# Low parts of the MLP and output weights stored in DRAM ahead of use, and two copies of x written later, in a fused attention and MLP kernel

## The chip, the cores and the metric

The kernel runs on one core of a Trainium2 chip. The metric is the device time of one execution in microseconds (us). An engine is one of five: PE (TensorE, the matrix engine), DVE (VectorE), ACT (ScalarE), POOL (GpSimd) and SP (SyncE, which here issues every DMA). Each engine runs its own instructions strictly in the order in which they stand in its queue and waits on semaphores for the others.

## The reference

A layer with x of 2048 rows and 640 columns (16 tiles of 128 rows, four blocks b = 0..3 of 512 rows), 32 heads of 20 columns, an attention window of 256 positions, and an MLP of width 1536 whose activation is a squared ReLU:

```python
x = A_x
xn = _layernorm(x, axis=-1)
s = _A_ref(xn, A_wqkv, A_wo)
g = _silu(_B_ref(xn, B_w1, B_b1, B_w2, B_b2))
return x + s * g
```

`_A_ref` is `softmax(mask(q k^T / sqrt(20))) v`, then the product with `wo`. `_B_ref` is `h = x w1 + b1`, `h = max(h, 0)^2`, `h w2 + b2`.

## The kernel before

Every product is made of parts. A float32 operand is split into a high part, which is a rounded copy made by ACT, and a low part, which is the difference raw minus high, made by a subtraction; a product is then high by high, high by low and low by high, three matmuls. So each weight exists twice in SBUF, as `hi` and `lo`.

**First stage (0 to 118 us of the profile).** For each block b of x: the products for q and k of the first head group (`qk_group`, L200), the next block's normalisation, transposes and split into `xT[0]` and `xT[1]`, and then the value products of all heads, `v_all` (L242). `v_all(b)` makes eight tiles t0..t7 of 15 matmuls each. A tile takes one of three PSUM buffers in turn (t6 has the buffer of t3), and ACT and DVE empty it: ACT L246 copies the high part `vt<-vps`, DVE L247 subtracts (`r<-vps,vt`), and after both the buffer is free; ACT L250 and DVE L251 make the two lower parts. `spill_x(b)` (L160) writes both parts of a block of x to the DRAM copies `xs`, 1280 KB each, since SBUF's place for x is given up before the MLP has used all of it. Stores of a tile are put in `stores`, and `store_all` posts them. In block 3, eight `pair_loads` (L403, 240 KB each) fetch q and k of the first pair of heads back in another layout, just before `v_all(3)`.

**Steps (118 to about 845 us).** Sixteen pairs of heads by 16 query tiles give 256 steps, and a few more to drain. Step s computes the scores of tile s (`sps`, L431), their maxima on DVE (L443), and 9 steps later (`LAG`) the transposed scores (`stps`, L475) with the maxima folded in as additional rows of the operand `qs`. Those rows (`mrow`) are made once for every four tiles (`max_rows`, L461) and reach `qs` by two small DMAs (`post`, L541). The transposed scores of step 9 are the first that read the rows of tiles 0 to 3, those of step 11 the first that read the rows of tiles 4 to 7. Then come the exponentials (ACT L482), the window's selection (POOL L483, L485), a high copy `ph` (ACT L490), a low part `pl` (DVE L496), and the product with the values (`ops`, L510).

**Filler.** Between these, PE gets filler in fixed portions: q and k products of the later head groups (`qkps`, L561), the MLP's first products (`hps`, L561) and second products (`yps`, L823), for half 0 of the MLP's width with blocks n = 0..3 and for half 1 with blocks n = 4..7, and at the end the output products (`wops`). The weights of the filler come in pieces (`piece_lin`, `piece_pair`): a DMA of the raw piece (L643), at least two steps later ACT's copy (L655 for w1 and w2, L663 for q, k and wo) and DVE's subtraction (L658, L664). `tick` releases one piece in a step, `ensure` releases what is left, `issue` starts pieces and, after them, the DMAs of the list `bulk` at a rate per step.

**What sets the order.** In the first stage a scheduler interleaves the engines' instructions; from the first step on (`manual_schedule`) the instructions stand in the order in which the code is written. SP issues DMAs in one order of its own, and eight semaphores go round: a DMA is issued only after the one eight places before it is done.

Of the kernel before, what the change touches and what calls it, by code (L numbers as in the profile page):

```python
# [51 lines left out]
def attn_mlp_kernel(ctx: ExitStack, tc, x, wqkv, wo, w1, b1, w2, b2, out):  # L52
# [15 lines left out]
    def qk_stores(w, rows, cols, hm, lo):  # L68
# [4 lines left out]
        rep = [hm[:, a, :].unsqueeze(1).to_broadcast([P, 3 - a, n]) for a in range(2)]  # L73
        return [(dst[:, 0:3, :], rep[0]), (dst[:, 3:5, :], rep[1]), (dst[:, 5, :], lo)]
    v_d = dram.tile([P, NP, NB, 4 * 2 * VW], BF16, name="v_d")
    y_d = [dram.tile([P, NT, D], F32, name=f"y{i}") for i in range(2)]
    o_d = [dram.tile([4, P, D], F32, name=f"o_{g}") for g in range(NB)]

# [48 lines left out]
    with tc.tile_pool(name="ph1v", bufs=2) as p1v, tc.tile_pool(name="ph1", bufs=2) as p1, tc.tile_pool(name="ph1x", bufs=4) as p1b, tc.tile_pool(name="ph1w", bufs=1) as p1w:  # L127
# [62 lines left out]
        def store_all():  # L190
            for dst, src in stores:
                nc.sync.dma_start(dst, src)
            stores.clear()
# [21 lines left out]
        def norm_jobs(b):  # L215
# [9 lines left out]
                    load_x(b + 1)  # L225
            return [lambda: None] + [lambda t=t: stats(xts[b][t], mv[:, t, :]) for t in range(4)] + [lambda: norm(0), lambda: norm(2)]

        def v_all(b, between=None):
            late = []
            jobs = norm_jobs(b + 2) if b + 2 < NB else []  # L230
            for nh in range(2):
                if nh and between:
                    between()
                vt = p1v.tile([P, NP // 2, 4, 2, VW], BF16, tag="vt", name="vt")
                nc.gpsimd.memset(vt[:, :, :, :, VW - 1:VW], 1.0)
                for t in range(4):
                    ps = pmm.tile([P, HALF], F32, tag="mm", name="vps")
                    n = 0
                    for c in range(KC):
                        for xp, wp in ((0, 0), (0, 1), (1, 0)):  # L240
                            n += 1
                            nc.tensor.matmul(ps, xT[xp][b][:, c * BT + t * P: c * BT + (t + 1) * P], wv[wp][:, c, nh * HALF:(nh + 1) * HALF], start=n == 1, stop=n == 3 * KC)  # L242
# [3 lines left out]
                    nc.scalar.activation(dst[:, :, :, 0:DH], psv, AF.Copy)  # L246
# [12 lines left out]
                late.pop()()  # L259
                stores.append((v_d[:, nh * (NP // 2):(nh + 1) * (NP // 2), b, :], vt.rearrange("p a t h w -> p a (t h w)")))  # L260

        E_ = mybir.EngineType
        with tc.manual_schedule(engines={E_.PE, E_.Activation, E_.DVE, E_.Pool, E_.SP}):
# [103 lines left out]
            for b in range(NB):  # L367
                def next_x():
                    if b + 1 < NB:
                        alloc_x(b + 1)  # L370
                        transpose_chunks(b + 1, xns)
                        xns.clear()
                        store_all()
                        spill_x(b + 1)

                if b == 0:
                    inv_std(rstd1, mv1[:, :, 1])
                    xns = [normalize(xts[1][t], mv1[:, t, :], rstd1[:, t:t + 1]) for t in range(4)]
                    load_x(2)
                    spill_x(0)  # L380
                    nc.sync.dma_start(b1t, b1.rearrange("(c p) -> p c", p=P))
                    nc.sync.dma_start(b2t, b2.partition_broadcast(P))
                    ones_rows(0)
                    raws = [load_w(group_src(1, w), KC) for w in "qk"]
                    v_all(b, next_x)
                    continue
                lasts = []
                for w in "kq":
                    ps = pmm.tile([P, BT], F32, tag="mm", name="qkps")
                    qk_group(w, b, ps)  # L390
                    lasts.append(qk_evac(w, b, ps))
                for f in lasts:
                    f()
                next_x()
                if b == 1:
                    for w in "qk":
                        ws1[w] = group_tiles(1, w)
                        split_w(*ws1[w], raws.pop(0))
                if b == NB - 1:
                    store_all()  # L400
                    for half in range(2):
                        for dst, src in pair_loads(0, half):
                            nc.sync.dma_start(dst, src)  # L403
                v_all(b)
            store_all()


    at1 = ctx.enter_context(tc.tile_pool(name="at1", bufs=1))
# [121 lines left out]
        return rest  # L530


    state = [0.0, 0.0, 0]
    posts = []

    def post(dst, src):
# [35 lines left out]
    def lin1(tiles, off, n):  # L572
        t, o = divmod(off, KC * BT)
        return tiles[t][:, o:o + n]
# [54 lines left out]
    def ensure(tag):  # L629
        flush()  # L630
        while any(p[0] == tag for p in started) or any(p[0] == tag for p in queue):
            start_pieces()
            for f in release(1, True):
                f()
                held[0] -= 1

    def piece(tag, src, go):
        def start():
# [7 lines left out]

    RAWN = {"g": D, "1": FHALF, "2": D, "o": D}

    def piece_lin(tag, tiles, ohi, olo, src):
        n = src.shape[-1]  # L650

        def go(raw):
            t_ = tiles()
            for ap, o, m in lin(t_, ohi, n):
                nc.scalar.activation(ap, raw[:, o:o + m], AF.Copy)  # L655
            cuts = sorted({o for o in range(0, n + 1, P) if (ohi + o) % (KC * BT) == 0 or (olo + o) % (KC * BT) == 0} | {0, n})
            for c0, c1 in zip(cuts, cuts[1:]):
                nc.vector.tensor_sub(lin1(t_, olo + c0, c1 - c0), raw[:, c0:c1], f32(lin1(t_, ohi + c0, c1 - c0)))  # L658
        piece(tag, src, go)

    def piece_pair(tag, hi, lo, src):
        def go(raw):
            nc.scalar.activation(hi(), raw, AF.Copy)  # L663
            nc.vector.tensor_sub(lo(), raw, f32(hi()))  # L664
        piece(tag, src, go)

    def lazy(make):
        got = []
# [17 lines left out]
    def queue_w1(hf):  # L686
        wt = lazy(lambda: [bigp.tile([P, KC * BT], F32R, tag="big", name=f"w1_{hf}_{j}") for j in range(3)])
        for c in range(KC):
            piece_lin(f"1{hf}", wt, c * FHALF, (KC + c) * FHALF, w1[c * P:(c + 1) * P, hf * FHALF:(hf + 1) * FHALF])
        return wt  # L690

    def queue_w2(hf):
        wt = lazy(lambda: [bigp.tile([P, KC * BT], F32R, tag="big", name=f"w2_{hf}_{j}") for j in range(3)])
        for j in range(NFH):
            piece_lin(f"2{hf}", wt, j * D, (NFH + j) * D, w2[hf * FHALF + j * P:hf * FHALF + (j + 1) * P, :])
        return wt

    def load_xb(b):
# [4 lines left out]
    def filler():  # L703
# [50 lines left out]
        for n, (hf, b) in enumerate(blocks):  # L754
            if n % NB == 0:
                ensure(f"1{hf}")
            if n == NB - 1:
# [38 lines left out]
            if n == NB:  # L796
                load_yin(0)
            wt2 = w2t[hf]()
            for tt in range(4):
                t = b * 4 + tt  # L800
                ysb = wgt.tile([P, D], F32, tag="wgqh", name="ysb")
# [30 lines left out]
                if n == last and tt % 2:  # L832
                    load(0)
                    load(1)
            if n == NB - 1:
                shut.discard("21")
        ensure("o")
# [20 lines left out]
    def queue_wo():  # L858
        wob = lazy(lambda: [bigp.tile([P, KC * BT], F32R, tag="big", name=f"wo{j}") for j in range(2)])
        wo4 = lazy(lambda: [wgt.tile([P, FHALF], F32R, tag="wraw", bufs=RAW, name=f"wo4{w}")[:, :D] for w in "hl"])  # L860

        def wo_part(p, c):
            return wob()[p][:, c * D:(c + 1) * D] if c < 4 else wo4()[p]

        for c in range(KC):
            piece_pair("o", lambda c=c: wo_part(0, c), lambda c=c: wo_part(1, c), wo[c * P:(c + 1) * P, :])
        return wo_part

    def out_filler(wo_part):
# [79 lines left out]
    per = total / (steps - 1)  # L949
    with tc.manual_schedule(engines={E_.PE, E_.Activation, E_.DVE, E_.Pool, E_.SP}):  # L950
        load_v(0)
        exs, phs, norm, loads = {}, {}, [], []

        def at_step(n):
# [2 lines left out]
        for s in range(steps):  # L957
# [40 lines left out]
                exs[b] = (exps(*b, *stp), stp[1])  # L998
            if c:
                high(*c, *exs.pop(c))  # L1000
            while norm:
                norm.pop()()
            fill((1 - EARLY_FILL) * per + SWING * (-1) ** (s - LAG - 3))
# [36 lines left out]
```

## Time and profile before

| | |
|---|---|
| median of 3 runs | 929.25 us (929.11 to 930.05) |
| profiled execution, its own time | 928.72 us |
| its span in the profile | 927.0 us |
| first stage, products of the last value block end at | 118.1 us |
| granted TensorE clock | 1.0 |

Times in the profile start at the span's first instruction. "Busy" of an engine is the time in which an instruction of its ran; idle time is put down to what released the engine afterwards. A window is a stretch of the span, with the busy time of each engine and the number of its instructions, the granted clock, the share of the 16 DMA engines' time and the bytes moved. A group is all instructions of one line, engine and operation, with their count, sum, mean duration, and the idle time just before them.

### The profile page before, as it was taken

The numbers are of one execution on the slowest core, as the hardware profiler recorded it, in microseconds if no ns is written. First come the engines' busy times: TensorE is split into PE (matmuls) and PEld (weight loads), VectorE is DVE, ScalarE is ACT, GpSimd is POOL, SyncE is SP. The second block draws the span as 40 slices with busy tenths as digits, with TensorE's granted clock in tenths as the row PEclk, the third lists the DMA queues.
The fourth block names the chain that finished last, engine by engine and source line by source line (L and its number), as shares of the span: only waits on it lengthen the run. The fifth ranks groups of instructions, "written<-read, shape, count | busy, mean of one in ns | idle before, by whom it ended". The sixth has DMA issues, their size and how long they took to land.

```text
span 927.0 us, 21775 instructions
## 1 busy us (share of the span) xinstructions
PE 902.9 (97%) x7632; PEld 728.9 (79%) x7632; DVE 754.8 (81%) x2031; ACT 670.1 (72%) x1282; POOL 530.0 (57%) x832
## 2 busy tenths in 40 slices
PE   8999999999998899999999999999999999999998
PEld 8999976666675578688688678688788687789998
DVE  7875478989989988988888899987888988875554
ACT  5454349888988886987986987977987977984221
POOL 6010017887877875775865875875864965871000
PEclk9999999999999999999999999999999999999999
DMA  6899776776778453253255143365274264055873
GB/s 230 279 398 338 229 249 203 224 240 213 237 234 258 120 187 112 88 181 117 72 180 166 52 149 122 101 222 157 53 253 129 74 220 134 24 189 172 287 277 114
DMA packets 130803, 168.79 MB, mean 182 GB/s; under 512 B 44100, under 2 KB 91268, under 8 KB 128132
## 3 DMA queue, kind: packets, MB, share of 16 engines
q1 hardware_dynamic: 130692, 167.39, 55.3%
q8 instruction: 60, 0.98, 0.4%
q14 instruction: 51, 0.42, 0.2%
HBM read 96.15 MB, written 70.91 MB: 180 GB/s over the span
## 4 chain that ended last, share of the span: by engine, by line
PE 74%; DVE 10%; ACT 5%; issue 4%; DMA 3%; POOL 3%; SPq 1%; POOLq 0%; DVEq 0%; ACTq 0%
PE yps L823 15%; PE hps L561 13%; PE wops L561 8%; PE vps L242 7%; PE qkps L561 7%; PE sps L431 7%; PE ops L510 7%; PE stps L475 6%; DVE junk L443 3%; PE qkps L200 2%; ACT p L482 2%; DVE pl L496 2%; DVE w L658 2%; ACT ph L490 1%; PE otp L889 1%
## 5 line engine op out<-in xcount | busy, mean ns | idle before, releaser
L482 ACT ACTIVATE p<-stps,ebias 128x384 f32<-128x384 f32 (+2 forms) x512 | 258.3, 557 | 82.6 <-PE stps L475 69.4
L443 DVE CUSTOM_DVE_ANT_0 junk<-sps,mask 128x384 bf16<-128x384 f32 (+2 forms) x512 | 251.1, 527 | 62.4 <-PE sps L431 55.2
L496 DVE TENSOR_TENSOR pl<-p,ph 128x768 f16<-128x768 f32 (+2 forms) x256 | 241.3, 943 | 2.6 <-ACT ph L490 2.2
L483 POOL TENSOR_SCALAR_AFFINE_SELECT p<-p 128x256 f32<-128x256 f32 x256 | 146.4, 572 | 136.2 <-ACT p L482 131.3
L490 ACT ACTIVATE ph<-p 128x768 f16<-128x768 f32 (+2 forms) x256 | 206.0, 805 | 15.1 <-POOL p L485 13.3
L561 PE MATMUL hps<-xb,w 128*128 128x512 f32 x630 | 198.2, 430 | 0.0
L823 PE MATMUL yps<-w,hh 128*128 128x320 f32 x768 | 197.6, 330 | 0.0
L823 PEld LDWEIGHTS yps<-w,hh 128*128 128x128 f32 x768 | 132.1, 189 | 8.1 <-issue 1.5
L431 PE MATMUL sps<-ks,qs 120*128 120x384 bf16 (+2 forms) x512 | 127.5, 319 | 8.9 <-DVE mt L443 8.8
L561 PEld LDWEIGHTS hps<-xb,w 128*128 128x128 f32 x630 | 113.3, 189 | 21.2 <-issue 0.4
L475 PE MATMUL stps<-qs,ks 122*128 122x384 bf16 (+2 forms) x512 | 124.4, 322 | 3.2 <-ACT p L482 2.1
L823 PE MATMUL yps<-w,hl 128*128 128x320 f32 x384 | 126.6, 330 | 0.0
L782 POOL TENSOR_TENSOR hl<-sq,hh 128x256 fp32r<-128x256 f32 x96 | 104.3, 1087 | 39.1 <-DVE sq L781 27.5
L510 PEld LDWEIGHTS <-ph 128*128 128x128 f16 x1440 | 86.0, 97 | 26.4 <-issue 21.5
L485 POOL TENSOR_SCALAR_AFFINE_SELECT p<-p 128x256 f32<-128x256 f32 x224 | 106.0, 473 | 0.0
L510 PE MATMUL ops<-vp,ph 128*128 128x61 bf16 x1440 | 101.0, 192 | 0.0
L510 PE MATMUL ops<-vp,pl 128*128 128x61 bf16 x1440 | 99.7, 191 | 0.0
L510 PEld LDWEIGHTS <-pl 128*128 128x128 f16 x1440 | 87.8, 97 | 0.0
L823 PEld LDWEIGHTS yps<-w,hl 128*128 128x128 f32 x384 | 72.4, 189 | 5.0 <-issue 2.0
L475 PEld LDWEIGHTS <-ks 122*128 122x128 bf16 x512 | 30.1, 99 | 55.7 <-issue 45.6
L242 PE MATMUL vps<-wv,xT 128*128 128x320 f32 x480 | 72.1, 309 | 0.6 <-POOL wv L179 0.3
L242 PEld LDWEIGHTS vps<-wv,xT 128*128 128x128 f32 x480 | 70.5, 187 | 1.3 <-POOL wv L179 0.6
(116 smaller groups left out, 1476.8 us busy)
## 6 DMA issues: line engine op xcount, KB each, us to landing
ks<-k_d SPq DMA_DIRECT2D x64, 240.0 KB
qs<-q_d SPq DMA_DIRECT2D x64, 240.0 KB
xb<-xs SPq DMA_DIRECT2D x12, 1280.0 KB
xs<-xT SPq DMA_DIRECT2D x8, 1280.0 KB
y<-ysb SPq DMA_DIRECT2D x32, 320.0 KB
q_d<-shm SPq DMA_DIRECT2D x38, 256.0 KB
v_d<-vt SPq DMA_DIRECT2D x8, 976.0 KB
vp<-v_d SPq DMA_DIRECT2D x16, 488.0 KB
```

The costliest lines, as they stand in the source:

```text
L242: nc.tensor.matmul(ps, xT[xp][b][:, c * BT + t * P: c * BT + (t + 1) * P], wv[wp][:, c, nh * HALF:(nh + 1) * HALF], start=n == 1, stop=n = ...
L431: nc.tensor.matmul(ps[:, :nk], qs[i][0:KR, hh, q * P:(q + 1) * P], ks[i][0:KR, hh, k0 * P:k0 * P + nk], start=True, stop=True)
L443: nc.vector.tensor_tensor_reduce(out=junk[:, :nk], in0=r[hh][:, :nk], in1=mask[:, 3 * P - nk:], scale=1.0, scalar=-3.0e38, op0=ALU.add, op ...
L475: nc.tensor.matmul(ps[:, :n], ks[i][0:KR + 2, hh, kb * P:(kb + 1) * P], qs[i][0:KR + 2, hh, kb * P:kb * P + n], start=True, stop=True)
L482: nc.scalar.activation(p32[:, hh, :n], r[hh][:, :n], AF.Exp, scale=SCALE, bias=ebias)
L483: nc.gpsimd.affine_select(p32[:, :, 0:P], p32[:, :, 0:P], pattern=[[0, 2], [1, P]], compare_op=ALU.is_ge, fill=0.0, base=0, channel_multip ...
L485: nc.gpsimd.affine_select(p32[:, :, 2 * P:], p32[:, :, 2 * P:], pattern=[[0, 2], [-1, P]], compare_op=ALU.is_gt, fill=0.0, base=0, channel ...
L490: nc.scalar.activation(ph[:, :, :n], p32[:, :, :n], AF.Copy)
L496: nc.vector.tensor_sub(pl[:, :, :n], p32[:, :, :n], ph[:, :, :n])
L510: nc.tensor.matmul(ot[:, q % 4, hh, :], t[:, hh, (q - k) * P:(q - k + 1) * P], vp[:, k // 4, k % 4, hh, :], start=m == 1, stop=m == 2 * le ...
L561: nc.tensor.matmul(ps, a, b_, start=j == 0, stop=j == n - 1)
L823: nc.tensor.matmul(pss[nh], hs[fc][hp][:, tt * P:(tt + 1) * P], lin1(wt2, (wp * NFH + fc) * D + nh * HALF, HALF), start=fc == 0 and j == 0 ...
```

## The change

The low parts of w1, w2 and wo are no longer subtracted where the filler uses them. They are made earlier, stored in three DRAM tensors, and read from there by a DMA straight into the `lo` place. The high parts are still loaded raw and copied by ACT. The weights of q and k keep their subtraction.

```diff
+    w1lo_d = [dram.tile([P, KC, FHALF], F32, name=f"w1lo{hf}") for hf in range(2)]
+    w2lo_d = [dram.tile([P, NFH, D], F32, name=f"w2lo{hf}") for hf in range(2)]
+    wolo_d = dram.tile([P, KC, D], F32, name="wolo")
...
             for ap, o, m in lin(t_, ohi, n):
                 nc.scalar.activation(ap, raw[:, o:o + m], AF.Copy)
-            cuts = sorted({o for o in range(0, n + 1, P) if (ohi + o) % (KC * BT) == 0 or (olo + o) % (KC * BT) == 0} | {0, n})
-            for c0, c1 in zip(cuts, cuts[1:]):
-                nc.vector.tensor_sub(lin1(t_, olo + c0, c1 - c0), raw[:, c0:c1], f32(lin1(t_, ohi + c0, c1 - c0)))
+            for ap, o, m in lin(t_, olo, n):
+                post(f32(ap), lo_d[:, o:o + m])
...
+    def piece_low(tag, hi, lo, src, lo_d):
+        def go(raw):
+            nc.scalar.activation(hi(), raw, AF.Copy)
+            post(f32(lo()), lo_d)
+        piece(tag, src, go)
```

The low parts of half 0 (12 pieces of 128 by 640, 320 KB each) are made in the first stage, one after each tile of `v_all(2)` (eight) and of the first four tiles of `v_all(3)`. Each loads a piece two ahead, copies on ACT, subtracts on DVE and stores.

```diff
+        def low_split():
+            if lraws:
+                raw, dst = lraws.pop(0)
+                hi = p1b.tile([P, D], F32R, tag="xn", name="whi")
+                lo = p1b.tile([P, D], F32R, tag="xn", name="wlo")
+                nc.scalar.activation(hi, raw, AF.Copy)
+                nc.vector.tensor_sub(lo, raw, f32(hi))
+                stores.append((dst, like(f32(lo), dst)))
+                low_load()
...
                     store_all()
+                    if b >= 2:
+                        low_split()
...
+                if b == 2:
+                    for _ in range(2):
+                        low_load()
                 v_all(b)
```

Those of half 1 (12) and of wo (5) are made among the steps, during the second products of blocks n = 0..2 and n = 4..6, with the subtraction on GpSimd. `low_tick` runs once a step; what is left at block 3 or 7 is made at once by `ensure_lows`.

```diff
+    def low_split():
+        _, raw, dst = lraws.pop(0)
+        hi = wgt.tile([P, FHALF], F32R, tag="wraw", bufs=RAW, name="whi")[:, :D]
+        nc.scalar.activation(hi, f32(raw), AF.Copy)
+        nc.gpsimd.tensor_sub(raw, f32(raw), f32(hi))
+        post(dst, like(f32(raw), dst))
+
+    def low_tick():
+        if lraws and state[2] >= lraws[0][0] + 3 and state[2] % 4 != 3:
+            low_split()
+        if state[3] and not lraws:
+            low_load()
...
+            if n in (NB - 1, last):
+                ensure_lows()
```

The copies of blocks 2 and 3 of x (four DMAs of 1280 KB) leave the first stage and go into the list `bulk` ahead of the first step.

```diff
-                        spill_x(b + 1)
+                        if b == 0:
+                            spill_x(b + 1)
...
         load_v(0)
+        for b_ in range(2, NB):
+            for p_ in range(2):
+                bulk_dma(1.8, xs_d[p_][b_], f32(xT[p_][b_]))
```

**ACT, the last value block.** Before, ACT's queue there held only the evacuations of the eight tiles (`vt<-vps`, then `vt<-r` for the lower part); these are its rows from t0 on:

```order
L246 ACTIVATE vt<-vps 128x8x2x20 x2
L250 ACTIVATE vt<-r_1355 128x8x2x20
L246 ACTIVATE vt<-vps 128x8x2x20
L250 ACTIVATE vt<-r_1374 128x8x2x20
L246 ACTIVATE vt<-vps 128x8x2x20
L250 ACTIVATE vt<-r_1395 128x8x2x20
```

Now the copies `whi` of the last four pieces of half 0 (pieces 8 to 11, counted from 0) stand between them, each waiting for its load `wraw`:

```order
L281 ACTIVATE vt<-vps 128x8x2x20
L258 ACTIVATE whi<-wraw 128x640
L281 ACTIVATE vt<-vps 128x8x2x20
L285 ACTIVATE vt<-r_1416 128x8x2x20
L258 ACTIVATE whi<-wraw 128x640
L281 ACTIVATE vt<-vps 128x8x2x20
L285 ACTIVATE vt<-r_1441 128x8x2x20
L258 ACTIVATE whi<-wraw 128x640
L281 ACTIVATE vt<-vps 128x8x2x20
L285 ACTIVATE vt<-r_1469 128x8x2x20
L258 ACTIVATE whi<-wraw 128x640
```

The first copy of t3 (the fourth `vt<-vps`) is now queued behind the third `whi`, that of piece 10.

**SP, the same place.** These are SP's rows now from the end of the eight pair loads to the two stores of the values; before, the stores of the values followed the pair loads directly:

```order
L441 DMA qs_125<-q_d 120x1024
L250 DMA wraw<-in_B_w_dram 128x640
L208 DMA w2lo_85<-wlo 128x640
L250 DMA wraw<-in_B_w_dram 128x640
L208 DMA w2lo_85<-wlo 128x640 x3
L208 DMA v_d<-vt 128x8x488 x2
```

The loads of pieces 10 and 11 are the two `wraw`, behind all eight pair loads.

**SP, the start of the steps.** These were SP's rows from the load of the first pair's values (`vp`) to the first rows of maxima (`mrow`); `raw` are pieces of the q and k weights of the next head group:

```order
L419 DMA vp_1532<-v_d 128x1952
L643 DMA raw<-in_A_wqkv_dram 128x5x128 x2
L116 DMA ks_1520<-ones 2x16x256
L590 DMA ks_1520<-k_d 120x1024
L590 DMA qs_1519<-q_d 120x1024
L590 DMA ks_1520<-k_d 120x1024
L590 DMA qs_1519<-q_d 120x1024
L541 DMA q_d<-shm 128x2x512
L541 DMA q_d<-slo 128x512
L541 DMA q_d<-shm 128x2x512
L541 DMA q_d<-shm 128x512
L541 DMA qs_120<-mrow 2x4x128 x2
```

and these are they now:

```order
L461 DMA vp_1617<-v_d 128x1952
L632 DMA xs_2_74<-xT_2_758 128x2560
L686 DMA raw<-in_A_wqkv_dram 128x5x128 x2
L632 DMA xs_2_78<-xT_2_759 128x2560
L132 DMA ks_1605<-ones 2x16x256
L632 DMA xs_3_75<-xT_3_1058 128x2560
L583 DMA q_d<-shm 128x2x512
L583 DMA q_d<-slo 128x512
L583 DMA q_d<-shm 128x2x512
L583 DMA q_d<-shm 128x512
L632 DMA xs_3_79<-xT_3_1059 128x2560
L583 DMA qs_125<-mrow 2x4x128 x2
```

All four copies of x stand ahead of the first `mrow`, one of them ahead of `raw`; the four loads of the second pair (`ks`, `qs`) stand behind it, ahead of the second `mrow`.

**DVE, the first weight pieces of the MLP.** Before, a subtraction `w<-raw,w` stood between the low part of the exponentials (`pl`) and the maxima of the next step:

```order
L496 TENSOR_TENSOR pl<-p_4233,ph 128x768
L658 TENSOR_TENSOR w_0_2_4230<-raw,w_0_0_4228 128x768
L443 ISA junk,mt<-sps,mask 128x384
L443 ISA mt 128x1
L443 ISA junk,mt<-sps,mask 128x384
L443 ISA mt 128x1
```

and at the same step now:

```order
L538 TENSOR_TENSOR pl<-p_4321,ph 128x768
L485 ISA junk,mt<-sps,mask 128x384
L485 ISA mt 128x1
L485 ISA junk,mt<-sps,mask 128x384
L485 ISA mt 128x1
```

The subtraction is gone, and the maxima follow `pl` directly.

More of the change, by code (lines that the diff above doesn't have):

```diff
@@ L226, in norm_jobs, with low_load @@
             return [lambda: None] + [lambda t=t: stats(xts[b][t], mv[:, t, :]) for t in range(4)] + [lambda: norm(0), lambda: norm(2)]
+        lows, lraws = mlp_lows(0), []
+        def low_load():
+            if lows:
+                src, dst = lows.pop(0)
+                raw = p1b.tile([P, D], F32, tag="xt", name="wraw")
+                nc.sync.dma_start(like(raw, src), src)
+                lraws.append((raw, dst))
+        def low_split():
[7 more added lines that the diff above has]
+                low_load()
         def v_all(b, between=None):
@@ L403, in attn_mlp_kernel @@
                             nc.sync.dma_start(dst, src)
+                if b == 2:
+                    for _ in range(2):
+                        low_load()
                 v_all(b)
             store_all()
+            assert not lraws
     at1 = ctx.enter_context(tc.tile_pool(name="at1", bufs=1))
@@ L635, in ensure @@
                 held[0] -= 1
+        post_all()
     def piece(tag, src, go):
@@ L647, in attn_mlp_kernel, with piece_lin @@
     RAWN = {"g": D, "1": FHALF, "2": D, "o": D}
-    def piece_lin(tag, tiles, ohi, olo, src):
+    def piece_lin(tag, tiles, ohi, olo, src, lo_d):
         n = src.shape[-1]
@@ L665, in piece_pair, with low_load, ensure_lows @@
         piece(tag, src, go)
+    def piece_low(tag, hi, lo, src, lo_d):
[3 more added lines that the diff above has]
+        piece(tag, src, go)
+    lows, lraws = [], []
+    def low_load():
+        if lows:
+            src, dst = lows.pop(0)
+            raw = wgt.tile([P, FHALF], F32R, tag="wraw", bufs=RAW, name="raw")[:, :D]
+            post(like(f32(raw), src), src)
+            lraws.append((state[2], raw, dst))
+    def low_split():
[9 more added lines that the diff above has]
+            low_load()
+    def ensure_lows():
+        while lows or lraws:
+            if not lraws:
+                low_load()
+            post_all()
+            low_split()
+        post_all()
     def lazy(make):
@@ L756, in filler @@
                 ensure(f"1{hf}")
+            if n == 0:
+                lows.extend(mlp_lows(1))
+            if n == NB:
+                lows.extend((wo[c * P:(c + 1) * P, :], wolo_d[:, c, :]) for c in range(KC))
+            if n in (NB - 1, last):
+                ensure_lows()
             if n == NB - 1:
@@ L798, in filler @@
             wt2 = w2t[hf]()
+            state[3] = n not in (NB - 1, last)
             for tt in range(4):
```

18 lines of the change are left out of this document (14 added, 4 removed).

## The prediction

> **What bounds the kernel now.** I read the page first: the busy shares, then the chain of work that ended last.
>
> ```profile
> span 927.0 us, 21775 instructions
> PE 902.9 (97%) x7632; PEld 728.9 (79%) x7632; DVE 754.8 (81%) x2031; ACT 670.1 (72%) x1282; POOL 530.0 (57%) x832
> PE 74%; DVE 10%; ACT 5%; issue 4%; DMA 3%; POOL 3%; SPq 1%; POOLq 0%; DVEq 0%; ACTq 0%
> ```
>
> PE is busy for 902.9 of 927.0 us, so all its idle time together is 24 us. No edit here changes PE's work, so the change can win only from those 24 us, and loses wherever it makes PE wait. The question is which of the idle time belongs to the subtractions that leave DVE. The second view is therefore the table of windows around the weight pieces:
>
> ```profile
> core 0: us, PE busy (x) PEld busy (x) DVE busy (x) ACT busy (x) POOL busy (x), PEclk, DMA share, GB/s
> 240.00:270.00 30.00, 30.00 (x274) 21.28 (x273) 27.63 (x75) 25.22 (x48) 23.51 (x35) 1.00 0.75 242
> 270.00:300.00 30.00, 26.00 (x215) 17.36 (x213) 28.48 (x65) 26.61 (x48) 21.47 (x29) 1.00 0.77 242
> 300.00:320.00 20.00, 17.13 (x141) 11.41 (x142) 19.90 (x47) 18.09 (x37) 16.10 (x20) 1.00 0.42 131
> 350.00:510.00 160.00, 159.80 (x1496) 127.04 (x1495) 136.51 (x407) 126.56 (x244) 104.54 (x181) 1.00 0.40 128
> 540.00:560.00 20.00, 17.68 (x167) 14.78 (x164) 19.93 (x50) 16.48 (x29) 14.68 (x21) 1.00 0.48 147
> 580.00:600.00 20.00, 18.71 (x163) 12.79 (x163) 19.86 (x53) 19.12 (x39) 16.70 (x23) 1.00 0.40 117
> ```
>
> At 240 to 270 and 350 to 510 PE has next to no idle time. In the four windows where pieces of w1 and w2 are split, DVE is full (28.48 of 30, 19.90, 19.93 and 19.86 of 20) and PE is idle for 4.00, 2.87, 2.32 and 1.29 us: 10.5 us. The waits of PE and the subtraction's share of these windows:
>
> ```profile
> PE sps L431 <- DVE mt L443: 5.2, 9, 1.2
> PE sps L457 <- DVE mp L448: 1.7, 3, 0.7
> 270.00:300.00 30.00, 7.56 (x7) 1.00 0.77 242
> 300.00:320.00 20.00, 6.93 (x6) 1.00 0.42 131
> 540.00:560.00 20.00, 5.97 (x7) 1.00 0.48 147
> 580.00:600.00 20.00, 4.32 (x4) 1.00 0.40 117
> ```
>
> The first two rows are PE's waits from 270 to 320: 6.9 us, all for DVE's maxima, in pieces of at most 1.2 us. The other four are DVE's busy time of the subtraction (L658) alone: 24.8 us in the four windows.
>
> **The gain (G).** 26 subtractions of w1 and w2 leave DVE, at 1035 ns each:
>
> ```profile
> L658 DVE TENSOR_TENSOR w<-raw,w 128x640 fp32r<-128x640 f32 (+3 forms) x26 | 26.6, 1035 | 0.0
> L655 ACT ACTIVATE w<-raw 128x640 fp32r<-128x640 f32 (+3 forms) x24 | 17.4, 734 | 1.0 <-DMA raw<-in_B_w_dram 1.0
> ```
>
> DVE's relief (24.8 us) exceeds what PE idles there (10.5), so the relief itself is not the limit. The next limit is ACT, whose copies stay: it idles 3.39, 1.91, 3.52 and 0.88 us in the four windows, and a window can shrink by no more than the smaller of PE's and ACT's idle time: 3.39 + 1.91 + 2.32 + 0.88 = 8.5 us. With the little that PE idles beyond these windows the bounds are 7 and 10.5; I take **G = 9.0**. The subtractions of wo are not on the path: PE is the full engine there, so nothing is counted.
>
> **The value products (A).** PE's rows of `v_all(2)` and `v_all(3)`, and the DMA traffic of the first of them:
>
> ```profile
> 75.80 17.85 PE L242 MATMUL vps<-wv,xT 128*128 128x320 f32 x120
> 100.35 17.76 PE L242 MATMUL vps<-wv,xT 128*128 128x320 f32 x120
> 64.00:84.00 20.00, 20.00 (x127) 18.72 (x126) 13.57 (x29) 9.34 (x21) 0.80 (x2) 1.00 1.06 393
> 80.00:98.00 18.00, 18.00 (x114) 17.20 (x113) 7.14 (x17) 6.91 (x16) 0.39 (x1) 1.00 0.66 253
> ```
>
> A tile takes 17.8 / 8 = 2.2 us. In `v_all(2)` DVE and ACT have room for eight splits (7.14 and 6.91 busy of 18 us). The queue moved 253 GB/s x 18 us = 4.6 MB from 80 to 98; 2.6 MB of x leave it, eight loads and eight stores of 0.33 MB bring 5.2 MB, together 7.2 MB, or 398 GB/s, against 393 in the fullest window quoted. So it just fits: 0 to 3 us, I take 0.5.
>
> In `v_all(3)` the load of piece 10 stands behind the eight pair loads, and ACT's copy of tile t3 behind the copy of that piece.
>
> ```profile
> 104.99 0.46 SPq L403 DMA_DIRECT2D ks<-k_d  x1
> 108.47 0.42 SPq L403 DMA_DIRECT2D qs<-q_d  x1
> 111.44 0.38 SPq L192 DMA_DIRECT2D v_d<-vt  x1
> DMA  9999999797796988889999999999998421000000
> GB/s 348 330 351 348 333 274 271 195 230 108 108 210 225 323 318 271 292 328 353 343 312 350 346 334 353 383 320 317 303 298 254 137 85 37 7 0 0 0 0 0
> L663 ACT ACTIVATE wgkh<-raw 128x640 fp32r<-128x640 f32 x3 | 2.3, 751 | 0.0
> 109.34 0.46 ACT L246 ACTIVATE vt<-vps 128x320 bf16<-128x320 f32 x1 [1.38 <-PE vps L242]
> 113.74 0.45 ACT L246 ACTIVATE vt<-vps 128x320 bf16<-128x320 f32 x1 [1.61 <-PE vps L242]
> ```
>
> The first three rows are SP issuing the first and the last pair load and the values' store (1.0 MB) behind them; the next two are the DMA engines from 104 to 120 in slices of 0.4 us. The queue is full until 116 and empty at 118. Counting 1.0 MB back from its end puts the end of the pair loads between 113.6 (all of the tail is the store) and 116. Piece 10 takes the store's place: 0.33 MB at about 0.33 MB/us is 1.0 us, so it lands at 114.6 to 117, I take 116. Then come ACT's copy (0.75), DVE's subtraction, which stands ahead of t3's on DVE (1.03), and t3's own subtraction (about 0.5): t3's PSUM buffer is free at 118.3. The last ACT row, at 113.74, is the emptying of t5: PE has finished t5 there and wants that buffer for t6. PE waits 118.3 - 113.7 = 4.6; **A = 4.5 + 0.5 = 5.0**, between 0 (piece 10 lands before 111.5) and 8. Before, t3 was emptied from 109.34 on, so this wait is wholly new. The first scores stand two tiles earlier on PE now, but cost only what they did. Late values also move the store `v_d`, and with it the start of the next part, by the same amount.
>
> **The start of the steps (B).**
>
> ```profile
> xs<-xT SPq DMA_DIRECT2D x8, 1280.0 KB
> 120.00:138.00 18.00, 17.48 (x82) 12.24 (x80) 14.48 (x50) 6.15 (x10) 3.50 (x3) 1.00 0.95 301
> DMA  0069999989999999999968899999999999995038
> 136.90 1.28 SPq L541 DMA_DIRECT2D qs<-mrow  x2
> 138.12 0.50 PE L475 MATMUL stps<-qs,ks 122*128 122x384 bf16 x2
> 142.82 0.50 PE L475 MATMUL stps<-qs,ks 122*128 122x384 bf16 x2
> ```
>
> The second row is the window from 120 to 138, the third the DMA engines from 120 to 140 in slices of 0.5 us. The queue is full from 121.5 on and drains at 138.2, just after the second rows of maxima were issued (136.90). PE needs the first rows at 138.12 (step 9) and the second at 142.82 (step 11), so before there were 4.6 us to spare for the second. Now four copies of 1.31 MB, 5.24 MB, stand ahead of both in SP's order. At 393 GB/s they take 13.3 us; the second rows land at 138.2 + 13.3 = 151.5, and PE waits 151.5 - 142.8 = **8.7 us = B** in all, part of it already at step 6 (the `raw` of the q weights is a copy later, and DVE's subtraction of it stands ahead of the maxima) and at step 9. If the old traffic too ran at 393 GB/s, 5.4 + 5.24 MB would need 27 us from 120.5 on, and the wait would be about 5; if the copies ran at 301, 17.4 us, and 12.8. Nothing makes this good later: PE is the full engine afterwards, and its filler is dealt out in a fixed order.
>
> On such an order the Trainium skill says, under "DMA: Bandwidth & Descriptors", section "Queues, rings and completion order", that descriptors of one issuer's queue are consumed in ring order on each DMA engine, but that completion is not first in, first out across engines, so that a small DMA may be done while a large earlier one still runs. By the first half B stands; by the second it would be near 0 if the few bytes of `mrow` went to engines that are done with their share of the copies. Of the trace, the full row of digits (9 in nearly every slice) shows all 16 engines loaded alike, which speaks for the first.
>
> **Splits among the steps (C).** 17 splits add 734 ns of ACT and one subtraction of POOL each.
>
> ```profile
> L179 POOL TENSOR_TENSOR wgkl<-raw,wgkh 128x640 fp32r<-128x640 f32 x2 | 3.4, 1708 | 6.3 <-DMA raw<-in_A_wqkv_dram 6.3
> L663 ACT ACTIVATE wo4h<-raw 128x640 fp32r<-128x640 f32 x1 | 0.7, 739 | 1.0 <-DMA raw<-in_A_wo_dram 1.0
> ```
>
> That is 12 x 0.73 = 9 us of ACT and 20 us of POOL within 350 to 510, where they idle 33 and 55 us while PE is full: hidden, as long as each load is in when ACT comes to it. One isn't: the twelfth piece of half 1 is loaded and copied at once. The nearest row is ACT's wait of 1.0 for a raw piece; bounds 0.5 and 3, **C = 1.5**. 27 low pieces come by DMA in place of a subtraction, 0.33 MB each; I count nothing for them, but their cover is that DMA has room at 270 to 320 (third rival).
>
> **Sum.** 928.7 (the profiled execution's own time) - 9.0 + 5.0 + 8.7 + 1.5 = 934.9. The median lies 0.5 above that execution, so I forecast **935.4 us**, 0.7% slower.
>
> **The rivals.**
>
> *Faster: the queue has room.* If DMA takes the additional traffic at its best rate everywhere, B is 5 or less and A about 1; G may be 10.5: 929.25 - 10.5 + 5 + 1 + 0.5 = 925. For it: before, the queue drained before every consumer, and 120 to 138 moved only 301 GB/s. Against it: the share there was already 0.95. It decides for faster once A + B falls below 7. Chance 0.16, times 921 to 927.4.
>
> *No difference.* The loads of pieces 10 and 11 land early (A near 1) and B stays at 7 to 8: 929.25 - 9 + 1 + 7.5 + 1.5 = 930. For it: the low end of the window of landing times above. Chance 0.12.
>
> *Slower still: the low parts come late.* From 270 to 320 the queue moved 242 x 30 + 131 x 20 GB/s = 9.9 MB; the low parts of half 0 add 12 x 0.33 = 3.9 MB. 13.8 MB need 35 us at 393 GB/s and 46 at 301, of 50. At the second rate the products `hps` and `yps` wait for DMA where scores waited for DVE, and G is used up: 944. For it: share 0.77 in the busier part. Against it: a piece is read a few steps after it is asked for. Chance 0.12, times 941 to 946.
>
> *The subtractions weren't the bound.* DVE is full there with maxima and `pl` too; if ACT fills up sooner than its idle time says, G is 3 and the time 941. Within the last case's range; it has a part of the forecast's upper end.
>
> **How the numbers follow.** The forecast's own case, 931.1 to 941, has 0.60. A measurement of this kernel tells 0.2%, 1.9 us, from no change: faster 0.16, same 0.12, slower 0.72. The range that leaves out 0.2: 925 (half of the faster case below it) to 942.5 (most of the slowest above it).
>
> **What would show each step.** G: the windows around the weight pieces have DVE below full, and PE's waits for the maxima (6.9 us) are nearly gone. A: PE idle in front of t6, put down to DVE or ACT behind `whi`. B: PE idle at the transposed scores of steps 9 and 11 until `mrow` lands, and a full row of DMA digits to about 150. C: ACT waiting for the last raw piece of half 1. I am wrong if PE is busy without a gap from 118 to 150, or if PE waits from 270 to 320 as before.

## The result, and the profile after

| | before | after |
|---|---|---|
| median of 5 runs | 929.5 us (929.11 to 930.05) | 944.7 us (942.3 to 946.55) |
| profiled execution, its own time | 928.72 us | 942.30 us |
| its span | 927.0 us | 940.6 us |

The ratio is 1.0163, with a 95% interval of 1.0152 to 1.0174: 1.6% slower. The forecast was 935.4 us, 0.7% slower, with a range to 942.5: the direction is right, but the forecast size is less than half of the measured one, and the time lies above the range. The page after, in the lines that were shown of before:

```profile
span 940.6 us, 21946 instructions
PE 907.6 (96%) x7632; PEld 733.2 (78%) x7632; DVE 746.3 (79%) x2012; ACT 683.9 (73%) x1311; POOL 549.1 (58%) x849
PE 77%; ACT 6%; DVE 6%; DMA 6%; SPq 2%; issue 2%; POOL 1%; ACTq 0%; POOLq 0%; DVEq 0%
```

DVE's share of the chain fell from 10% to 6%, as it should without the subtractions; DMA's rose from 3% to 6%. PE runs as many instructions, but was busy for 907.6 instead of 902.9 us: 4.7 us more for the same work. The windows of the two places that were forecast to lose say why, in their column PEclk:

```profile
core 0: us, PE busy (x) PEld busy (x) DVE busy (x) ACT busy (x) POOL busy (x), PEclk, DMA share, GB/s
80.00:98.00 18.00, 18.00 (x115) 17.27 (x114) 10.09 (x20) 8.38 (x18) 0.39 (x1) 1.00 0.95 305
114.00:122.00 8.00, 0.62 (x4) 0.19 (x2) 0.85 (x2) 1.48 (x4) 0.00 (x0) 0.66 0.95 328
122.00:126.00 4.00, 3.57 (x13) 3.57 (x14) 3.25 (x7) 2.21 (x5) 0.00 (x0) 0.50 0.46 176
140.00:160.00 20.00, 15.39 (x64) 10.29 (x62) 10.49 (x36) 8.95 (x14) 5.14 (x7) 0.91 1.03 388
```

PE stands still for nearly all of 114 to 122, and runs at half its clock for some 4 us afterwards. The other thing to see is the first row: beside the values of block 2 the share of the DMA engines' time is 0.95, but they move 305 GB/s, not the 393 that the forecast took.

Where the time went is best read from PE, since the order of its instructions is the same in both kernels but for two scores. The start of the same PE instruction in the two profiles, us:

| PE instruction | before | after | later by | in this part |
|---|---|---|---|---|
| last matmul of `v_all(3)` | 117.80 | 128.77 | 10.97 | **+10.97** (A) |
| transposed scores of step 11 | 142.82 | 162.44 | 19.62 | **+8.65** (B) |
| scores of step 60 | 273.64 | 293.05 | 19.41 | -0.21 |
| scores of step 80 | 336.22 | 352.71 | 16.49 | **-2.92** (half 0's weights) |
| scores of step 140 | 497.43 | 514.43 | 17.00 | +0.51 |
| scores of step 148 | 518.69 | 537.63 | 18.94 | **+1.94** (C) |
| scores of step 180 | 609.25 | 624.35 | 15.10 | **-3.84** (half 1's weights) |
| last transposed scores | 836.33 | 850.32 | 13.99 | -1.11 |

**A** is 11.0 where 5.0 was forecast. Four rows of after show its chain, from SP (the first pair load, and the load of piece 10), ACT (the copy of piece 10) and PE (tiles t6 and t7):

```profile
109.57 0.57 SPq L441 DMA_DIRECT2D ks<-k_d  x1
113.84 0.37 SPq L250 DMA_DIRECT2D wraw<-in_B_w_dram  x1
120.38 0.74 ACT L258 ACTIVATE whi<-wraw 128x640 fp32r<-128x640 f32 x1 [11.96 <-DMA wraw<-in_B_w_dram]
122.43 6.64 PE L277 MATMUL vps<-wv,xT 128*128 128x320 f32 x30 [6.12 <-DVE r L282]
```

The kind of wait is the forecast one: ACT waits 11.96 us for the load of piece 10, t3 isn't emptied meanwhile, and PE waits 6.12 us for DVE's subtraction of t3. But the pair loads go out at 109.57 instead of 104.99, so everything behind them is 4.6 us late. And the 30 matmuls take 6.64 us, where a quarter of the 17.76 for 120 is 4.44: 2.2 us for the clock. The 6.12 us are not all of the wait: just before, PE does the first two scores, 0.23 us each, and waits 1.7 us in front of them for the late pair loads. In all, t6 begins at 122.43, where before it began at 113.55: 8.9 us later, and with the clock's 2.1 to 2.2 that is the 11.0.

Why the pair loads are late can be read in rows of SP and ACT beside block 2, and in the window in which SP comes to the second half of the values:

```profile
89.78 0.38 SPq L208 DMA_DIRECT2D v_d<-vt  x1
90.20 0.68 SPq L250 DMA_DIRECT2D wraw<-in_B_w_dram  x1
98.15 0.74 ACT L258 ACTIVATE whi<-wraw 128x640 fp32r<-128x640 f32 x1 [4.44 <-DMA wraw<-in_B_w_dram]
99.78 0.33 SPq L208 DMA_DIRECT2D w2lo<-wlo  x1
101.81 0.38 SPq L208 DMA_DIRECT2D v_d<-vt  x1
98.00:102.00 4.00, 4.00 (x23) 3.49 (x22) 3.07 (x6) 3.52 (x7) 0.00 (x0) 1.00 0.76 243
```

The load of piece 6 (`wraw`) goes out at 90.20, right behind the 1.0 MB store of half the values (`v_d`), and ACT waits 4.44 us for it. Behind this wait stand, on ACT and DVE, the emptying of the block's last tiles and, in SP's order, the store of the piece's low part (`w2lo`): SP issues nothing from 96.8 to 99.78. So the store of the other half of the values goes out at 101.81, where before it went out at 95.78, and the stores of q and k and the pair loads stand behind it. From 98 to 102 the DMA engines had room (0.76).

**B** is 8.65 where 8.7 was forecast. The waits of PE from 112 to 165 (the first and the fourth row belong to A), then its transposed scores of steps 9 and 11:

```profile
PE vps L277 <- DVE r L282: 6.1, 1, 6.1
PE stps L517 <- DMA qs<-mrow: 4.6, 2, 2.9
PE sps L473 <- DVE mt L485: 2.8, 2, 2.4
PE sps L473 <- DMA qs<-q_d: 1.7, 2, 1.2
154.65 0.57 PE L517 MATMUL stps<-qs,ks 122*128 122x384 bf16 x2 [1.67 <-DMA qs<-mrow]
162.43 0.53 PE L517 MATMUL stps<-qs,ks 122*128 122x384 bf16 x2 [2.94 <-DMA qs<-mrow]
```

The waits are those forecast, at step 6 for the maxima and at steps 9 and 11 for `mrow`, and the window from 140 to 160 moved 388 GB/s at a full share, where the sum had taken 393 for the copies. The three waits are 7.0 us; the other 1.6 are lost between steps 6 and 8, where PE's clock is halved behind the first of them.

**C**, and a wait that the forecast had given to a rival, in ACT's rows at 305 and 523 us, and in a window of PE behind the first of them:

```profile
305.81 0.84 ACT L698 ACTIVATE w<-raw 128x768 fp32r<-128x768 f32 x1 [2.41 <-DMA raw<-in_B_w_dram]
523.59 0.74 ACT L728 ACTIVATE whi<-raw 128x640 fp32r<-128x640 f32 x1 [3.28 <-DMA raw<-in_B_w_dram]
308.00:312.00 4.00, 4.00 (x15) 2.65 (x13) 2.51 (x7) 3.48 (x7) 3.48 (x6) 0.60 1.01 369
```

At 523 ACT waits 3.28 us for the piece that is loaded and copied at once: 1.9 us are lost. At 305 it waits 2.41 us for a raw piece of w1, which is late in a full queue (share 1.01 in the window behind it); PE waits for the exponentials behind it, and its clock is halved after. Between steps 64 and 68 the kernel loses 2.9 us again that it had gained.

### The profile page after: what moved, and what is told of

It is laid out like the page before. It is cut to its first block, busy times and chain, and to the rows that moved or that the text cites. A ratio compares the mean times of both kernels' runs of the same rounds, so it can differ in the third digit from the quotient of the medians.

```text
span 940.6 us, 21946 instructions
## 1 busy us (share of the span) xinstructions
PE 907.6 (96%) x7632; PEld 733.2 (78%) x7632; DVE 746.3 (79%) x2012; ACT 683.9 (73%) x1311; POOL 549.1 (58%) x849
## 4 chain that ended last, share of the span: by engine, by line
PE 77%; ACT 6%; DVE 6%; DMA 6%; SPq 2%; issue 2%; POOL 1%; ACTq 0%; POOLq 0%; DVEq 0%
PE yps L909 16%; PE hps L603 13%; PE qkps L603 8%; PE wops L603 8%; PE ops L552 7%; PE stps L517 7%; PE sps L473 7%; PE vps L277 7%; ACT p L524 3%; PE qkps L216 2%; DMA raw<-in_B_w_dram 2%; DVE junk L485 2%; ACT ph L532 1%; DMA qs<-mrow 1%; DVE pl L538 1%
## 5 line engine op out<-in xcount | busy, mean ns | idle before, releaser
L538 DVE TENSOR_TENSOR pl<-p,ph 128x768 f16<-128x768 f32 (+2 forms) x256 | 250.0, 977 | 5.7 <-ACT ph L532 5.7
L525 POOL TENSOR_SCALAR_AFFINE_SELECT p<-p 128x256 f32<-128x256 f32 x256 | 133.0, 520 | 108.3 <-ACT p L524 101.7
L527 POOL TENSOR_SCALAR_AFFINE_SELECT p<-p 128x256 f32<-128x256 f32 x224 | 103.1, 460 | 0.0
L277 PE MATMUL vps<-wv,xT 128*128 128x320 f32 x480 | 74.3, 314 | 6.7 <-DVE r L282 6.1
L277 PEld LDWEIGHTS vps<-wv,xT 128*128 128x128 f32 x480 | 72.5, 192 | 7.5 <-DVE r L282 6.3
```

What stands on the lines that cost most here:

```text
L525: nc.gpsimd.affine_select(p32[:, :, 0:P], p32[:, :, 0:P], pattern=[[0, 2], [1, P]], compare_op=ALU.is_ge, fill=0.0, base=0, channel_multip ...
L538: nc.vector.tensor_sub(pl[:, :, :n], p32[:, :, :n], ph[:, :, :n])
```

## The experiments

In the expectations "the first loss" is A, "the start of the steps" B.

**e1, the copies of x later.**

```diff
-        for b_ in range(2, NB):
-            for p_ in range(2):
-                bulk_dma(1.8, xs_d[p_][b_], f32(xT[p_][b_]))
...
             issue(RATE)
...
+            if s in (14, 17, 20, 23):
+                i_ = (s - 14) // 3
+                bulk_dma(1.8, xs_d[i_ % 2][2 + i_ // 2], f32(xT[i_ % 2][2 + i_ // 2]))
```

> The changed kernel with the four copies of x issued at steps 14, 17, 20 and 23 instead of ahead of the first steps; all else as changed. Theory (the copies ahead of the rows of maxima cost the 8.8 us that steps 4 to 12 lost): that loss falls to 1 or less, the rest stays, 944.7 - 8.5 = about 936. Rival (the loss there is the aftermath of the late end of the value products: the queue is behind anyway): most of it stays, 942 or more.

932.83 us (ratio 1.0035, 1.0023 to 1.0046). PE's transposed scores of step 11, and all its waits from 130 to 165:

```profile
153.57 0.50 PE L517 MATMUL stps<-qs,ks 122*128 122x384 bf16 x2
PE sps L473 <- DVE mt L485: 0.4, 1, 0.4
PE sps L499 <- DVE mp L490: 0.2, 1, 0.2
```

Step 11 is 10.75 later than before the change, as much as the first loss alone, and the waits for `mrow` are gone. So the start of the steps lost its 8.65 us to the four copies. The medians differ by 11.9 us, more than the 8.5 expected, the profiled executions by 9.6: 8.9 of these at step 11, 0.7 behind step 148. The rest is no saving in the profiles: the changed kernel's profiled execution was its fastest, 2.4 us below its median.

**e2, pieces 10 and 11 loaded ahead of the pair loads.**

```diff
                 if b == NB - 1:
                     store_all()
+                    low_split()
+                    low_split()
+                    store_all()
                     for half in range(2):
```

> The changed kernel with the splits of pieces 8 and 9 ahead of the eight pair loads, so that the loads of pieces 10 and 11 go out before the pair loads and the remaining two splits stand beside tiles t0 and t1. Theory of the order (the 11 us lost at the end of the value products come from piece 10 standing behind the pair loads): nearly all of it goes, about 935. Theory of the queue (the traffic beside the block before made the stores of q and k, and so everything behind them, 4.6 us late): ACT waits for piece 10 further up, and half stays, 938 to 941.

939.45 us (1.0108, 1.0092 to 1.0125). ACT's wait and PE's:

```profile
113.65 0.74 ACT L258 ACTIVATE whi<-wraw 128x640 fp32r<-128x640 f32 x1 [8.22 <-DMA wraw<-in_B_w_dram]
115.70 10.89 PE L277 MATMUL vps<-wv,xT 128*128 128x320 f32 x60 [5.87 <-DVE r L282]
```

The first loss falls only from 11 to 8.5. The load is in 6.7 us earlier, but ACT's copy of piece 10 now stands two tiles further up, ahead of t1, and PE waits 5.87 us there. So the theory of the queue had it: the order against the pair loads is not the cause by itself; a late piece in ACT's queue is.

**e3, the copies of x back in the first stage.**

```diff
-                        if b == 0:
-                            spill_x(b + 1)
+                        spill_x(b + 1)
...
-        for b_ in range(2, NB):
-            for p_ in range(2):
-                bulk_dma(1.8, xs_d[p_][b_], f32(xT[p_][b_]))
```

> The changed kernel with the copies of x for blocks 2 and 3 back where they were, in the first stage. Theory of the queue: 5.2 MB more before the value products make pieces and pair loads later by up to 13 us, the first loss grows from 11 to 17 to 24, while the 8.8 us at the start of the steps go: 942 to 950. Theory of the order: the first loss stays at 11, 936.

941.18 us (1.0124, 1.0109 to 1.0139).

```profile
92.29 10.62 PE L277 MATMUL vps<-wv,xT 128*128 128x320 f32 x60 [7.38 <-DVE r L282]
130.04 6.14 PE L277 MATMUL vps<-wv,xT 128*128 128x320 f32 x30 [5.90 <-DVE r L282]
```

Now both blocks of values wait, 7.38 and 5.90 us, and the last value product ends 18 us later than before. The first loss grew from 11 to 18 with the copies queued ahead of the pieces. That the changed kernel moves the copies away was right for its first stage; the place that it gave them was wrong.

**e4, no splits of half 0.** `mlp_lows(0)` is left out in the first stage, and `piece_lin` subtracts for half 0 as before:

```diff
-        lows, lraws = mlp_lows(0), []
+        lows, lraws = [], []
...
+            if tag[1] == "0":
+                cuts = sorted({o for o in range(0, n + 1, P) if (ohi + o) % (KC * BT) == 0 or (olo + o) % (KC * BT) == 0} | {0, n})
+                for c0, c1 in zip(cuts, cuts[1:]):
+                    nc.vector.tensor_sub(lin1(t_, olo + c0, c1 - c0), raw[:, c0:c1], f32(lin1(t_, ohi + c0, c1 - c0)))
...
```

> The changed kernel without the twelve splits of half 0 in the first stage; the low parts of half 0 are subtracted on DVE at their use, as before the change. Both theories: the first loss (11.0) goes, the net gain of half 0 (2.9) goes too, the start of the steps still costs 8 to 9: 944.7 - 11.0 + 2.9 = 936.6. If the start of the steps recovers too, its loss was an aftermath: 929.

934.29 us (1.0050, 1.0035 to 1.0065).

```profile
100.63 17.76 PE L277 MATMUL vps<-wv,xT 128*128 128x320 f32 x120
143.67 0.52 PE L517 MATMUL stps<-qs,ks 122*128 122x384 bf16 x2 [1.17 <-DMA qs<-mrow]
151.42 0.53 PE L517 MATMUL stps<-qs,ks 122*128 122x384 bf16 x2 [2.96 <-DMA qs<-mrow]
```

The first loss is gone, and the start of the steps costs 8.3 us without it (step 11 at 151.42, before 142.82, of which 0.3 stood there already). The two losses are separate causes.

**e10, only the four splits beside the last values.** `mlp_lows(0)[8:]`, split for b == 3 alone; the first eight pieces are subtracted on DVE as before.

```diff
-        lows, lraws = mlp_lows(0), []
+        lows, lraws = mlp_lows(0)[8:], []
...
-                    if b >= 2:
+                    if b == 3:
                         low_split()
...
```

> The changed kernel with only the four splits beside the last values (pieces 8 to 11); the first eight pieces of half 0 are subtracted on DVE, as before. The queue beside block 2's values is then emptier than before the change. If the lateness from that block made the first loss 11.0 instead of the 5 that I forecast, it is 4 to 6 here, with pair loads issued near 105. If the order in the last block alone makes the loss, it stays at 10 to 11.

938.33 us (1.0096, 1.0081 to 1.0111). The same four rows as for A above:

```profile
104.97 0.46 SPq L441 DMA_DIRECT2D ks<-k_d  x1
109.03 0.36 SPq L250 DMA_DIRECT2D wraw<-in_B_w_dram  x1
116.36 0.74 ACT L258 ACTIVATE whi<-wraw 128x640 fp32r<-128x640 f32 x1 [8.41 <-DMA wraw<-in_B_w_dram]
118.41 6.03 PE L277 MATMUL vps<-wv,xT 128*128 128x320 f32 x30 [4.60 <-DVE r L282]
```

This is the forecast's own chain, number by number: pair loads at 105, piece 10 in at 116, PE waits 4.6 us for t3. The 30 matmuls take 6.03 instead of 4.44, and by the table's measure, the last matmul of `v_all(3)`, the first loss is 6.3, just above the 4 to 6 expected. What the changed kernel has beyond that, 4.6 us, is the eight splits beside block 2, which make the pair loads and piece 10 late.

**e5, only the eight splits beside block 2.** `mlp_lows(0)[:8]`; the last four pieces of half 0 are subtracted on DVE.

```diff
-        lows, lraws = mlp_lows(0), []
+        lows, lraws = mlp_lows(0)[:8], []
...
```

> The changed kernel with only the eight splits beside the values of block 2; the last four pieces of half 0 are subtracted on DVE at their use, as before. Nothing of a split stands beside the last values. If the first loss (11.0) comes from ACT holding the tiles' emptying behind the late piece 10, it falls to 0 to 2 though the pair loads go out as late as in the changed kernel (about 109.6): 944.7 - 10 + 1.5 for four subtractions back = 936. If the late pair loads are themselves what PE waits for, 4 to 5 us of it stay: 939 to 941.

931.82 us (1.0024, 1.0015 to 1.0034). SP's first pair load, and PE's value products:

```profile
109.75 0.59 SPq L441 DMA_DIRECT2D ks<-k_d  x1
100.91 17.82 PE L277 MATMUL vps<-wv,xT 128*128 128x320 f32 x120
```

The pair loads are as late as in the changed kernel, and PE doesn't wait at all in the value products. So late pair loads cost nothing by themselves; they cost through the copy on ACT that stands ahead of t3. It came out 4 us lower than expected. The 1.5 allowed for four subtractions back on DVE was not needed: half 0's weights gain 2.9 net in both profiles. Of the rest, 1.6 us are gained behind step 148, from causes that no run separates, and 1 us is again the distance of the profiled executions from their medians.

**e6, e5 with the copies of x late (the edits of e5 and e1).**

> The same with the copies of x at steps 14, 17, 20 and 23. If the two losses are independent and add: 932.8 - 10 + 1.5 = 924, faster than before the change by 0.5%. If the time lost in the first stage comes back later in another wait: 929 or more.

923.48 us (0.9932, 0.9917 to 0.9946), where 924 was expected: the losses add, and without them the change is a gain over the kernel before.

**e7 and e8, two pieces loaded ahead among the steps**, with e1, and with e6:

```diff
-        if state[3] and not lraws:
+        if state[3] and (not lraws or len(lraws) == 1 and state[2] > lraws[0][0]):
             low_load()
```

> The changed kernel with the late copies of x (as e1) and, among the steps, two pieces loaded ahead instead of one, so that the twelfth piece of half 1 is no longer loaded and copied at once. Theory: ACT's wait for that load costs the 1.8 us lost near step 140: 932.8 - 1.8 = 931. Rival: it is the splits' own ACT and POOL time, which only moves: 932.8.

> All three together: eight splits only, late copies of x, two pieces loaded ahead among the steps. If the three savings add: 924 - 1.8 = 922. If they don't, the time of the run before it stays, 924.

945.74 us (1.0180) and 934.00 us (1.0051): both are slower by over 10 us than what they start from. ACT's waits in e7 from 340 to 460:

```profile
ACT whi L728 <- DMA w2lo<-raw: 7.1, 2, 3.9
ACT whi L728 <- POOL p L527: 5.0, 2, 2.6
```

`whi` takes one of three buffers, which it shares with the raw pieces. With two pieces loaded, it must wait until an older piece has been subtracted and stored. The wait for a load became a wait for a store, on the same engine and more often. This says nothing against the theory of C: between steps 140 and 148, where C lies, neither run loses anything. e9 tries it in another way.

**e9, e6 with eleven pieces of half 1**; the twelfth is subtracted on DVE.

```diff
-                lows.extend(mlp_lows(1))
+                lows.extend(mlp_lows(1)[:11])
...
```

> The fastest so far (eight splits beside the values, copies of x late), and only eleven splits of half 1 among the steps: the twelfth piece is subtracted on DVE at its use, as before, so nothing is loaded and copied at once. Theory: ACT's wait for that load costs the 1.9 us lost near step 140: 923.5 - 1.9 = 921.6. Rival: the cost is that of the splits' ACT and POOL time: 923.3.

919.9 us (0.9909, 0.9892 to 0.9925). Between steps 140 and 148 nothing is lost any more: C was ACT's wait for that load. The profiled executions of e6 and e9 differ by 2.1 us, of which 2.0 lie there; the medians, taken on two chips, by 3.6. This is the fastest version of all, 0.9% faster than the kernel before. Its page and all of PE's waits in it that come from the steps:

```profile
span 917.4 us, 21918 instructions
PE 901.0 (98%) x7632; PEld 728.6 (79%) x7632; DVE 747.2 (81%) x2013; ACT 681.6 (74%) x1306; POOL 550.7 (60%) x848
PE stps L517 <- ACT p L524: 3.8, 8, 1.2
PE sps L499 <- DVE mp L490: 2.6, 5, 1.3
PE sps L473 <- DVE mt L485: 0.5, 2, 0.3
270.00:300.00 30.00, 27.19 (x224) 18.54 (x223) 23.71 (x67) 27.90 (x51) 20.64 (x32) 1.00 1.00 327
```

PE's waits for the maxima, the largest before, are down to 0.5 us, and the largest now is for ACT's exponentials. In the last row ACT (27.90 of 30) is fuller than DVE (23.71).

## Why the prediction was right and wrong

**What bounds it, and the gain (G): right in the mechanism, in part by luck in the sum.** DVE's subtractions held PE, ACT is the next limit, and the gain is near the 9.0 forecast. The changed kernel shows 2.92 + 3.84 + 1.11 = 7.9; e9, with five pieces still on DVE, is 9.1 ahead at the last transposed scores. But the parts are not those of the sum. Half 0's weights give 2.9 net, where the two windows at 270 to 320 were to give 3.39 + 1.91 = 5.3; half 1's give 3.8 for 3.2. One part was counted as nothing and perhaps wasn't: in the last part, in which wo's pieces leave DVE, both gain 1.1 to 1.7; no run tried that by itself.

**Block 3's splits: right, in the case they were worked out for.** e10 has piece 10 at 116 and PE's wait at 4.6, the forecast's numbers. The 116 was chosen from a range of 114.6 to 117, so that it came out to a few tenths is luck. The first scores did not "cost only what they did": in the changed kernel they wait 1.7 us, though in the shadow of the wait for t3.

**Block 2's splits: this step failed.** The forecast put 7.2 MB in 18 us against 393 GB/s and wrote "So it just fits: 0 to 3 us, I take 0.5". It took the splits for bytes in a queue. The runs show a chain: a store of SP waits for DVE's subtraction, that for ACT's copy, that for a load, and the load was issued in the same order behind a 1.0 MB store. The mean of 305 GB/s at a share of 0.95 covers stretches of both kinds: 362 GB/s at 1.06 from 92 to 98, and 243 at 0.76 from 98 to 102, where SP mostly waited. From 102 on the queue is full again (1.02 to 112) and lets the stores of q and k out more slowly than before. The pair loads are 4.6 us late by it, and piece 10 with them; how much of that is SP's waiting and how much the full queue, no run separates. PE was never held in block 2 (18.00 of 18.00 busy), so the price showed up one block further on, in the term that had been worked out with the old times of issue. e10 (6.3) and the changed kernel (11.0) put it at 4.6, where the sum had 0.5, and e5 shows that the eight splits alone make the pair loads late.

**The clock: not in the sum at all.** A wait of PE was priced at its length. After the wait for t3 the next 30 matmuls took 2.2 us more (1.6 in e10). The Trainium skill, "TensorE: Matmul & The Clock Gate", section "What's actually happening", says that PE's clock is halved after an idle window of about 3.4 us and restored after as long a busy one. By that rule the wait of 4.6 us would have cost some 1.7 us more (an estimate from the page's figure: half of 3.4 us), and the trace agrees with such a price behind the long waits.

**B: right,** in its mechanism, its places and its size (8.65 of 8.7). In the four other kernels with the copies ahead of the steps (e2, e4, e5, e10) this part costs 8.3 to 8.7 us, in those without them 0.5 or less. **C: right** (1.94 of 1.5), and e9 shows that it is the wait for that load. The forecast's 27 low pieces are 29 in the trace; it counted nothing for them, so no sum changes.

**The third rival** (low parts and raw pieces late at 270 to 320 us) came in part. In the changed kernel it is one wait of 2.4 us, 2.9 with its clock. In e1, e5 and e9 ACT waits in that stretch too, at other places: 3.1, 2.7 and 2.9 us from 265 to 345, all for raw pieces; and half 0's weights give 2.6 to 3.3 net. That these waits are what G lacks there is likely, but no run tried it, nor whether they are why the changed kernel's times spread over 4 us.

## What to carry to other kernels

Bytes divided by a queue's rate are not the time of a chain of loads and stores that wait for engines. Before adding such a chain, go through the issuer's order entry by entry: which store waits for which engine, which load stands behind which large store, and which transfer that somebody waits for stands behind them all. A load that is waited for in the middle of an engine's queue costs what stands behind it there, so splits beside other work need their data in before the first of them, or a place where nothing urgent follows. And copies that nobody reads soon belong behind the small transfers that somebody waits for: four copies moved by a dozen steps were worth nearly 9 us.

## What the hardware showed unexpectedly

A short wait of PE can halve its clock. These are PE's waits in the changed kernel and the windows behind them:

```profile
144.04 0.96 PE L473 MATMUL sps<-ks,qs 120*128 120x384 bf16 x2 [2.43 <-DVE mt L485]
144.00:148.00 4.00, 3.96 (x12) 2.68 (x12) 2.79 (x8) 1.23 (x2) 0.94 (x2) 0.58 1.01 429
307.18 0.88 PE L517 MATMUL stps<-qs,ks 122*128 122x384 bf16 x2 [2.30 <-ACT p L524]
163.00:167.00 4.00, 4.00 (x21) 2.69 (x20) 2.33 (x7) 4.00 (x8) 2.52 (x3) 1.00 0.93 310
```

After waits of 2.43 and 2.30 us the granted clock was 0.58 over the 4 us from 144 and 0.60 over those from 308, while after the wait of 2.94 us before 162.43 it stayed at 1.00. In e1 a wait of 1.51 us, up to 319.28, was followed by 0.63 and 0.52 in the two stretches of 2 us from 320. The length of a wait alone doesn't decide. The Trainium skill says in the section named above that the window of about 3.4 us is free-running, which would fit that; but waits of 1.5 to 2.4 us are shorter than the idle window that it asks for, and no run here shows the window itself.

Transfers of 2 KB waited here for the whole queue ahead of them. `mrow` stands behind the four copies in SP's order, and step 11, which needs it, came 8.65 us late, where the sum for strict order gave 8.7; nothing was seen of small transfers passing large ones.
